# A decode kernel: query projection written to (head, batch) rows and spread by 4 products in place of 128, and a bias product from two bf16 parts

## Chip, cores, metric

One core of one Trainium2 chip. The metric is the device time of one execution in microseconds (us); lower is better. "Span" is the time from the first to the last instruction in a profile; it is some 1.5 us shorter than the device time.

## The reference, cut to what matters

```python
B, Sq, D = 4, 1, 640;  H, Sk, Dh = 32, 4096, 128;  F = 1728      # all bf16
q      = (layernorm(x) @ wq)  -> (B, H, 1, Dh)
scores = q . k_cache * Dh**-0.5                                   # k_cache, v_cache: (4, 32, 4096, 128)
o      = softmax(scores) . v_cache
h      = x + o.reshape(B, 1, H*Dh) @ wo
hid    = layernorm(h) @ w1 + b1
out    = h + mish(hid) @ w2
```

k_cache and v_cache are 134 MB each. With the weights, 283.35 MB have to be read once, and each byte is used for very little arithmetic.

## The kernel before

The caches are cut into 16 tiles of K and 16 of V (4 groups of 8 heads times 4 batches; 8.39 MB each, 128 partitions of 64 KB). They pass through three slots, A, B and C, in SBUF. Every large load is issued on one queue, by SyncE, as soon as its slot is free (x, b1 and one small piece of the weights are loaded through ScalarE's queue):

```python
def first_loads():
    load(sp, slot["C"][:, 0 : DC * H * Dh], ... A_wq ..., "wq", "WQ")    # 5.24 MB, in the slot of the first V
    ...
    k_load(0)                       # slot A
    k_load(1)                       # slot B

def sync_prog():
    for hg in range(NHG):
        ...
        sp.need(("PV", i - 1) if hg else ("qb", NHG - 1))    # the first V overwrites wq: wait for the projection
        v_load(i)
        sp.need(("F", i, NS - 1))   # fold of K tile i done: slot A is free
        k_load(i + 2)
        ...
```

VectorE multiplies a K tile by `q_bc` (q, repeated for all rows of its head), PE adds up over the head dimension (the "fold", with `ident` as weights), VectorE and ScalarE finish the scores, PE multiplies with V (`pv`).

The head of the program, which the change touches. wq is projected to `q_all`, rows (head group, batch), 1024 columns (8 heads by 128). Then, for each head group, batch and head, a product with a 0/1 matrix `sel` writes one head's q to the 16 rows that hold that head's keys:

```python
for h in range(2):
    for c in range(DC):
        for hg in range(NHG):
            o = hg * QN + h * 512
            mm(red[hg*QD : (hg+1)*QD, h, :], lnT[:, c, :], wq[:, c, o : o + 512], c == 0, c == DC - 1, ...)   # 40 products
pe.need(("qa", 0), ("qa", 1))            # two copies red -> q_all on ScalarE
for hg in range(NHG):
    for b in range(N):
        for g in range(G):               # 4 x 4 x 8 = 128 products
            mm(red[:, (2+hg) % 4, b*Dh : (b+1)*Dh], sel[r, b, SE - PG*g : SE - PG*g + P],
               q_all[r, g*Dh : (g+1)*Dh], g == 0, g == G - 1, ...)
# ScalarE: four copies red -> q_bc
```

The tail of the program, which the change touches as well. The bias b1 times the standard deviation is added to the first feed-forward product by one f32 product with an f32 identity, between the first and the second of three groups of w1 products:

```python
pe.need("cen")                           # centred h, bf16
for c0, c1 in zip(W1S, W1S[1:]):         # W1S = (0, 2, 4, 5)
    if c1 == DC - 1:
        pe.need("b1s")
        mm(red[:, 2, 0 : FC*N], ident_f[:, :], b1s[...], False, False)      # f32, 56 columns
    pe.need(("w1", c0))
    for j in ...: for c in range(c0, c1): mm(h1_ps[...], w1 piece, cen[:, c, :], ...)   # 28, 28 and 14 products
```

The softmax here doesn't subtract the row's maximum and nothing guards it: scores larger than these inputs give would overflow.

Of the kernel before, what the change touches and what calls it, by code (L numbers as in the profile page):

```python
# [7 lines left out]
FP32 = mybir.dt.float32  # L8
BF16 = mybir.dt.bfloat16
ACT = mybir.ActivationFunctionType  # L10
ALU = mybir.AluOpType
# [67 lines left out]
def kernel(  # L79
# [15 lines left out]
    N, _, D = A_x.shape  # L95
    _, H, Sk, Dh = A_k_cache.shape
    F = B_w1.shape[1]
    P = 128
    DC = D // P
    G = 8  # L100
    PG = P // G
    R = Sk // PG
    NS = 4
# [9 lines left out]
    CG = 4  # L113
# [59 lines left out]
    wq = slot["C"][:, 0 : DC * H * Dh].rearrange("p (c n) -> p c n", c=DC)  # L173
    x_bf = sb("x_bf", (N, D), BF16, setup, topC)
    ln1 = sb("ln1", (N, D), BF16, setup, topC)
    lnT = sb("lnT", (P, DC, QD), BF16, setup, topC)
    xT = sb("xT", (P, DC, N), BF16, setup, topC)
    q_all = sb("q_all", (P, QN), BF16, setup, topC)
    SE = P - PG
    sel_f = sb("sel_f", (P, N), FP32, setup, topC)  # L180
    sel = sb("sel", (P, N, SE + P), BF16, setup, topC)
    stats = sb("stats", (N, 2, nc.vector.BN_STATS_DIM), FP32, setup, topC)
    mv = sb("mv", (N, nc.vector.BN_AGGR_DIM), FP32, setup, topC)
    std = sb("std", (N, 1), FP32, setup, topC)
# [5 lines left out]
    tail = [sA + FM * D * 2]  # L190
    topA = sA + SLOT * 2
    ones_d = sb("ones_d", (P, P), FP32, tail, topA)
    ident_f = sb("ident_f", (P, P), FP32, tail, topA)
    zeros = sb("zeros", (P, OC), BF16, tail, topA)
    st = sb("st", (P, 2, DC, N), FP32, tail, topA)
    mu = sb("mu", (P, 2, N), FP32, tail, topA)
# [3 lines left out]
    std2 = sb("std2", (P, N), FP32, tail, topA)  # L200
    rstd = sb("rstd", (P, N), FP32, tail, topA)
    b1s = sb("b1s", (P, FC, N), FP32, tail, topA)
    h_hi = sb("h_hi", (P, DC, N), BF16, tail, topA)
    h_lo = sb("h_lo", (P, DC, N), BF16, tail, topA)
    act = sb("act", (P, FC, N), BF16, tail, topA)
# [90 lines left out]
    def sync_prog():  # L296
        for hg in range(NHG):
            i = hg * N
            if hg:
                sp.need(("PV", i - 2))  # L300
                k_load(i)
                sp.need(("F", i - 1, NS - 1))
                k_load(i + 1)
            sp.need(("PV", i - 1) if hg else ("qb", NHG - 1))
            v_load(i)
            sp.need(("F", i, NS - 1))
            k_load(i + 2)
            sp.need(("PV", i))
            v_load(i + 1)
            sp.need(("F", i + 1, NS - 1))  # L310
            k_load(i + 3)
            sp.need(("F", i + 2, NS - 1))
            v_load(i + 2)
            sp.need(("PV", i + 1))
            v_load(i + 3)
        sp.need(("F", NT - 1, NS - 1))
        for n, (q, j0, j1) in enumerate(WOS):
            load(
                sp, wo_sb[:, q, j0:j1, :],
                A_wo[q * QN : (q + 1) * QN, :].rearrange("(p j) n -> p j n", j=G)[:, j0:j1, :],  # L320
                ("wo", q, j0), f"W{n}",
            )
        w1_v = B_w1.rearrange("(p c) n -> p c n", c=DC)
        for k, (c0, c1) in enumerate(zip(W1S, W1S[1:])):
            load(sp, w1_sb[:, c0:c1, :], w1_v[:, c0:c1, :], ("w1", c0), f"W{len(WOS) + k}")
        sp.need(("PV", NT - 2))
        w2_v = B_w2[0 : FM * P, :].rearrange("(p j) n -> p j n", j=FM)
        for k, (j0, j1) in enumerate(zip(W2S, W2S[1:])):
            load(sp, w2_sb[:, j0:j1, :], w2_v[:, j0:j1, :], ("w2", j0), f"W{len(WOS) + len(W1S) - 1 + k}")
        store(sp, 0)  # L330
        leave(sp, 0)

    def pool_prog():
        g = nc.gpsimd
        po.do(lambda: g.memset(ident[:, :], 0.0), "id0", "PO")
        po.need("id0")
        po.do(
            lambda: g.affine_select(
                out=ident[:, :], in_=ident[:, :], compare_op=ALU.not_equal, fill=1.0, base=0,
                pattern=[[-1, P]], channel_multiplier=1,  # L340
            ),
            "ident", "PO",
        )
        po.do(lambda: g.memset(b1T[:, :], 0.0), "b1z", "PO")
        po.do(lambda: g.memset(lnT[:, :, :], 0.0), "lnz", "PO")
        po.do(lambda: g.memset(sel[:, :, :], 0.0), "selz", "PO")
        po.do(lambda: g.memset(selo[:, :, :], 0.0), "seloz", "PO")
        po.do(lambda: g.memset(ones[:, :], 1.0), "ones", "PO")
        po.need(("PV", NT - 2))
        po.do(lambda: g.memset(ones_d[:, :], 1.0 / D), "ones_d", "PO")  # L350
        po.do(lambda: g.memset(zeros[:, :], 0.0), "zeros", "PO")
        po.do(lambda: g.tensor_copy(out=ident_f[:, :], in_=ident[:, :]), "ident_f", "PO")

    def act_prog():
        a = nc.scalar
# [7 lines left out]
            ),  # L363
            "std", "AC",
        )
        for h in range(2):
            ac.need(("q", h))
            ac.do(
                lambda: a.copy(out=q_all[:, h * 512 : (h + 1) * 512], in_=red[:, h, :]),
                ("qa", h), "ACP",  # L370
            )
        for hg in range(NHG):
            ac.need(("qb", hg))
            ac.do(
                lambda: a.copy(
                    out=q_bc[:, hg, :, :].rearrange("p b d -> p (b d)"), in_=red[:, (2 + hg) % 4, :]
                ),
                ("qc", hg), "AC",
            )

        ac.need("ident")
# [52 lines left out]
    def dve_prog():  # L434
# [5 lines left out]
        for k in range(2):  # L440
# [3 lines left out]
        dv.need("ident")  # L444
        dv.do(
            lambda: v.tensor_reduce(
                out=sel_f[:, :],
                in_=ident[:, :].rearrange("p (h m) -> p m h", h=CG)[:, 0:N, :],
                axis=AX.X, op=ALU.add,
            ),  # L450
            "sel_f", DV,
# [28 lines left out]
            ),  # L480
            "selo", DVP,
        )
        dv.need("delta_f", "selz")
        dv.do(lambda: v.tensor_copy(out=hmask[:, :], in_=hmask_f[:, :]), "hmask", DV)
        dv.do(lambda: v.tensor_copy(out=delta[:, :], in_=delta_f[:, :]), "delta", DVP)
        dv.do(
            lambda: v.tensor_copy(
                out=sel[:, :, SE : SE + PG],
                in_=sel_f[:, :].unsqueeze(2).to_broadcast([P, N, PG]),
            ),  # L490
            "sel", DVP,
        )
# [8 lines left out]
            "ln1", DVP,  # L501
        )
        dv.need("tpl", "lnz")
        dv.do(lambda: v.tensor_copy(out=lnT[:, :, 0:N], in_=tpl[:, :, :]), "lnT", DVP)
        dv.need("tpx")
        dv.do(lambda: v.tensor_copy(out=xT[:, :, :], in_=tpx[:, :, :]), "xT", DVP)
        dv.do(lambda: v.memset(rsm[:, :, :], 1.0), ("rsm", -1), DVP)
        dv.need(("qc", NHG - 1), "hmask")

        def mult(i, s):  # L510
            hg, b = divmod(i, N)
# [109 lines left out]
        for k in range(2):  # L621
# [34 lines left out]
                out=b1s[:, :, :], in0=b1T[:, :].unsqueeze(2).to_broadcast([P, FC, N]),  # L656
                in1=std2[:, :].unsqueeze(1).to_broadcast([P, FC, N]), op=ALU.mult,
            ),
            "b1s", DVP,
        )  # L660
        dv.do(lambda: v.reciprocal(out=rstd[:, :], in_=std2[:, :]), "rstd", DV)
        dv.need("h_hi")
        dv.do(
            lambda: v.tensor_tensor(
                out=h_lo[:, :, :], in0=st[:, 0, :, :], in1=h_hi[:, :, :], op=ALU.subtract
            ),
            "h_lo", DVP,
        )
        dv.need("h1_ps", "rstd")
        dv.do(  # L670
# [59 lines left out]
    def pe_setup():  # L730
        pe.need("ident", "x", "delta", "ones")
        for c in range(DC):
            mm(
                tpx[:, c, :], x_bf[:, :].rearrange("n (p c) -> n c p", c=DC)[:, c, :],
                ident[0:N, 0:N], True, True, "tpx" if c == DC - 1 else None,
            )
        pe.need("ln1")
        for c in range(DC):
            mm(
                tpl[:, c, :], ln1[:, :].rearrange("n (p c) -> n c p", c=DC)[:, c, :],  # L740
                ident[0:N, 0:N], True, True, "tpl" if c == DC - 1 else None,
            )
        pe.need("xT")
        mm(y_full[:, 0 : DC * N], ident[:, :], xT[:, :, :].rearrange("p c n -> p (c n)"), True, False)
        pe.need("lnT", "wq")
        for h in range(2):
            for c in range(DC):
                for hg in range(NHG):
                    o = hg * QN + h * 512
                    mm(  # L750
                        red[hg * QD : (hg + 1) * QD, h, :], lnT[:, c, :], wq[:, c, o : o + 512],
                        c == 0, c == DC - 1,
                        ("q", h) if c == DC - 1 and hg == NHG - 1 else None,
                    )
        pe.need(("qa", 0), ("qa", 1))
        for hg in range(NHG):
            for b in range(N):
                for g in range(G):
                    r = slice(hg * QD, (hg + 1) * QD)
                    done = b == N - 1 and g == G - 1  # L760
                    mm(
                        red[:, (2 + hg) % 4, b * Dh : (b + 1) * Dh],
                        sel[r, b, SE - PG * g : SE - PG * g + P],
                        q_all[r, g * Dh : (g + 1) * Dh],
                        g == 0, g == G - 1, ("qb", hg) if done else None,
                    )

    def fold(i, s):
        t = slot[KS[i % N]][:, :].rearrange("p (r d) -> p r d", d=Dh)
# [76 lines left out]
    def pe_tail():  # L846
# [14 lines left out]
        l_mm(hg)  # L861
        wo_mm(1)
        a_mm(hg)
        pe.need("ident_f", ("e", NT - 1, NS - 1))
        mm(red[:, 2, 0 : FC * N], ident[:, :], zeros[:, 0 : FC * N], True, False)
        mm(y2_ps, ident[:, :], zeros[:, 0:OC], True, False)
        wo_mm(2)
# [8 lines left out]
            )  # L876
        pe.need("cen")
        for c0, c1 in zip(W1S, W1S[1:]):
            if c1 == DC - 1:
                pe.need("b1s")  # L880
                mm(
                    red[:, 2, 0 : FC * N], ident_f[:, :], b1s[:, :, :].rearrange("p j n -> p (j n)"),
                    False, False,
                )
            pe.need(("w1", c0))
            for j in [FM] + list(range(FM)):
                for c in range(c0, c1):
# [6 lines left out]
                        h1_ps[0 : (P if j < FM else FT), j, :], w, cen[:, c, :], False, done,  # L894
                        "h1_ps" if done else None,
                    )
        pe.need("h_lo")
        for part in (h_hi, h_lo):
            for k in range(CG):
                for c in range(DC):  # L900
# [89 lines left out]
```

## Time and profile before

663.92 us (median of 3 runs, 663.88 to 663.99); span 662.2 us.

| | before |
|---|---|
| busy share of the span: PE, VectorE, ScalarE | 60%, 61%, 6% |
| DMA, 36 to 636 us | share 1.00, 433 GB/s |
| q_bc complete / first product with K0 starts | 35.3 / 36.84 us |
| last half of the last V lands / its products start | 635.9 / 636.02 us |
| last piece of w2 lands / last result computed | 658.4 / 660.3 us |

Lines of the page of the profile. The first is busy time per engine. The next two cut the span into 40 slices: the clock granted to PE in tenths, and the busy share of the 16 DMA engines in tenths. Then come groups of instructions: line, engine, operation, output and inputs, count, busy time and mean ns, and after the second bar the idle time before them with what ended it.

```profile
...
PE 399.4 (60%) x2747; PEld 83.3 (13%) x1787; DVE 406.8 (61%) x252; ACT 41.6 (6%) x158; POOL 2.6 (0%) x14
...
PEclk9998698869659796869668778977965879786855
DMA  9999999999999999999999999999999999999997
...
L515 DVE TENSOR_TENSOR slotA<-slotA,q_bc 128x8192 bf16<-128x8192 bf16 x32 | 140.6, 4415 | 108.1 <-DMA slotA<-in_A_k_cache_dram 108.1
...
L708 PE MATMUL red<-q_all,sel 32*128 32x128 bf16 x128 | 12.5, 307 | 0.8 <-PEq L49 0.8
```

(The first clock record in this trace is at 46.8 us; the 9s that open its PEclk line stand for no record.) No compute engine is busy much more than 60% of the time, while the DMA engines are in the top tenth in every slice but the last. VectorE's products with K idle 108 us for the K tiles of slot A alone, and the profile puts all of it down to their DMA. The stretch from 36 to 636 us alone (columns: busy time of PE, PE weight load, VectorE, ScalarE, GpSimd, granted clock, DMA share, GB/s):

```profile
...
36.00:636.00 600.00, 359.24 (x2184) 50.30 (x1225) 398.61 (x213) 32.08 (x144) 0.61 (x3) 0.80 1.00 433
```

The Trainium skill ("DMA: Bandwidth & Descriptors", Specifications) gives 435 GB/s as the ceiling of the fabric; 433 over 600 us is within 0.5% of it.

Now the two places of the change. In the timeline (start, duration, engine, operation), the last copy to q_bc:

```profile
...
34.71 0.59 ACT L375 CAST q_bc<-red 128x512 bf16<-128x512 f32 x1 [2.38 <-PE red L708]
```

VectorE's first two products with K0, and what ended the idle time before them:

```profile
...
36.84 8.76 DVE L515 TENSOR_TENSOR slotA<-slotA,q_bc 128x8192 bf16<-128x8192 bf16 x2 [28.68 <-DMA slotA<-in_A_k_cache_dram]
```

The issue of the load of the first V (slot C) and of the third K (slot A):

```profile
...
34.70 0.33 SPq L250 DMA_DIRECT2D slotC<-in_A_v_cache_dram  x1
64.68 0.33 SPq L250 DMA_DIRECT2D slotA<-in_A_k_cache_dram  x1
```

q_bc was there 1.5 us before VectorE started; what it waited for was K0. In the tail, around the bias product (group of 28, bias weight load and product in two passes, groups of 28 + 14, and the step that takes the result):

```profile
...
636.02 3.60 PE L708 MATMUL pv<-slotC,e 128*32 128x512 bf16 x32 [3.16 <-PEq L49]
...
650.60 1.92 PE L708 MATMUL red<-cen,slotB 128*64 128x4 bf16 x28
...
652.32 0.54 PEld L708 LDWEIGHTS red<-b1s,ident_f 128*128 128x128 f32 x2
652.38 0.66 PE L708 MATMUL red<-b1s,ident_f 128*128 128x56 f32 x2
...
652.97 2.98 PE L708 MATMUL red<-cen,slotB 128*64 128x4 bf16 x42
...
655.99 0.22 DVE L671 TENSOR_TENSOR h<-red,rstd 128x56 f32<-128x56 f32 x1 [4.29 <-PE red L708]
```

The chain that ended last (start, duration, what) holds in one piece the three groups and the bias:

```profile
...
635.98 0.04 issue
...
650.60 5.36 PE red L708 x72
```

Everything on that chain before 635.98 us is waiting for data; from there it is compute.

### The profile page before, as it was taken

How to read it: one execution, taken by the hardware profiler on the slowest of the kernel's cores; microseconds unless marked ns; L12 is line 12 of the kernel's file. 1: busy time of each engine (PE TensorE's matmuls, PEld its weight loads, DVE VectorE, ACT ScalarE, POOL GpSimd, SP SyncE). 2: the span in 40 equal slices, each digit the busy share in tenths (PEclk: the TensorE clock that was granted, in tenths of full speed). 3: DMA queues.
4: the chain of work that ended last, by engine and by line, in shares of the span. 5: the costliest groups of instructions: out<-in, count | busy, mean ns of one | idle time of the engine just before them, and what ended most of it. 6: DMA issues, size and time to landing. Idle time of an engine off the chain costs nothing. (4 is left out here: it accounts for less than half of the span.)

```text
span 662.2 us, 5205 instructions
## 1 busy us (share of the span) xinstructions
PE 399.4 (60%) x2747; PEld 83.3 (13%) x1787; DVE 406.8 (61%) x252; ACT 41.6 (6%) x158; POOL 2.6 (0%) x14
## 2 busy tenths in 40 slices
PE   0957666557317595838307485828534757675877
PEld 0710010101101010101100010100110001010147
DVE  1067889486048778677219688948306798858612
ACT  0110000000000000000000000000000000000011
POOL 1000000000000000000000000000000000000000
PEclk9998698869659796869668778977965879786855
DMA  9999999999999999999999999999999999999997
GB/s 385 437 443 413 420 444 433 444 435 436 421 432 439 428 443 435 439 420 435 439 428 435 443 439 420 435 439 424 439 439 443 420 435 435 428 439 439 412 419 289
DMA packets 6978, 283.50 MB, mean 428 GB/s; under 512 B 1012, under 2 KB 1208, under 8 KB 2232
## 3 DMA queue, kind: packets, MB, share of 16 engines
q1 hardware_dynamic: 6640, 283.27, 99.0%
q8 instruction: 7, 0.11, 0.1%
q10 hardware_dynamic: 328, 0.09, 0.1%
q14 instruction: 3, 0.02, 0.0%
HBM read 283.35 MB, written 0.01 MB: 428 GB/s over the span
## 5 line engine op out<-in xcount | busy, mean ns | idle before, releaser
L515 DVE TENSOR_TENSOR slotA<-slotA,q_bc 128x8192 bf16<-128x8192 bf16 x32 | 140.6, 4415 | 108.1 <-DMA slotA<-in_A_k_cache_dram 108.1
L515 DVE TENSOR_TENSOR slotB<-slotB,q_bc 128x8192 bf16<-128x8192 bf16 x32 | 140.7, 4417 | 17.0 <-DMA slotB<-in_A_k_cache_dram 17.0
L526 DVE TENSOR_REDUCE s_f<-red 128x64 f32<-128x1024 f32 x64 | 78.0, 1219 | 97.6 <-PE red L718 97.6
L718 PE MATMUL red<-slotA,ident 128*128 128x512 bf16 x480 | 135.9, 446 | 0.0
L718 PE MATMUL red<-slotB,ident 128*128 128x512 bf16 x480 | 127.9, 426 | 0.0
L708 PE MATMUL red<-slotA,ident 128*128 128x512 bf16 x32 | 14.3, 447 | 117.2 <-PEq L49 117.2
L708 PE MATMUL pv<-slotC,e 128*32 128x512 bf16 x768 | 53.1, 437 | 37.0 <-PEq L49 34.0
L708 PE MATMUL red<-slotB,ident 128*128 128x512 bf16 x32 | 14.1, 441 | 87.7 <-PEq L49 87.7
L394 ACT ACTIVATE ex<-s_f 128x64 bf16<-128x64 f32 x64 | 16.4, 256 | 503.2 <-DVE s_f L526 503.2
L540 DVE TENSOR_TENSOR e<-ex,hmask 128x512 bf16<-128x512 bf16 x64 | 39.8, 683 | 0.0
L708 PEld LDWEIGHTS pv<-slotC,e 128*32 128x32 bf16 x768 | 22.7, 108 | 94.1 <-issue 80.5
L708 PEld LDWEIGHTS red<-slotA,ident 128*128 128x128 bf16 x32 | 3.2, 99 | 184.7 <-issue 184.6
L708 PEld LDWEIGHTS red<-slotB,ident 128*128 128x128 bf16 x32 | 3.2, 99 | 171.9 <-issue 171.9
L708 PEld LDWEIGHTS o_ps<-pv_sb,selo 128*32 128x32 f32 x136 | 13.9, 113 | 65.0 <-issue 64.8
L708 PE MATMUL o_ps<-pv_sb,selo 128*32 128x128 f32 x136 | 18.9, 284 | 0.0
L708 PE MATMUL pv<-slotA,e 128*32 128x512 bf16 x256 | 14.6, 380 | 0.3 <-PEq L49 0.3
L404 ACT COPY pv_sb<-pv 128x512 f32<-128x512 f32 x16 | 9.4, 586 | 68.4 <-PE pv L708 68.4
L708 PE MATMUL red<-q_all,sel 32*128 32x128 bf16 x128 | 12.5, 307 | 0.8 <-PEq L49 0.8
L708 PEld LDWEIGHTS red<-q_all,sel 32*128 32x128 bf16 x128 | 12.2, 142 | 1.7 <-issue 1.7
L394 ACT ACTIVATION_READ_ACCUMULATOR ex<-s_f 128x1 f32 x64 | 11.9, 186 | 0.0
L708 PEld LDWEIGHTS pv<-slotA,e 128*32 128x32 bf16 x256 | 6.7, 97 | 23.4 <-issue 17.5
L708 PE MATMUL red<-slotC,lnT 128*32 128x512 bf16 x40 | 4.5, 629 | 8.5 <-PEq L49 8.5
(96 smaller groups left out, 74.3 us busy)
## 6 DMA issues: line engine op xcount, KB each, us to landing
slotC<-in_A_v_cache_dram SPq DMA_DIRECT2D x2, 4096.0 KB, 39.1
slotC<-in_A_wq_dram SPq DMA_DIRECT2D x1, 5120.0 KB, 15.9
slotB<-in_A_wo_dram SPq DMA_DIRECT2D x3, 1280.0 KB, 15.7
slotB<-in_B_w_dram SPq DMA_DIRECT2D x2, 864.0 KB, 22.8
slotB<-in_A_wo_dram SPq DMA_DIRECT2D x1, 960.0 KB, 20.1
slotA<-in_B_w_dram SPq DMA_DIRECT2D x1, 960.0 KB, 25.1
slotA<-in_B_w_dram SPq DMA_DIRECT2D x1, 640.0 KB, 22.3
slotB<-in_B_w_dram SPq DMA_DIRECT2D x1, 432.0 KB, 24.2
```

The source lines that it names most:

```text
L394: lambda: a.activation(out=ex[:, sl], in_=s_f[:, sl], func=ACT.Exp, scale=SCALE, accum_out=rs[:, b, s : s + 1],),
L404: lambda: a.copy(out=pv_sb[:, :, :].rearrange("p r d -> p (r d)"), in_=pv[:, :]),
L515: lambda: v.tensor_tensor(out=t, in0=t, in1=q_bc[:, hg, b, :].unsqueeze(1).to_broadcast([P, RS, Dh]), op=ALU.mult,),
L526: lambda: v.tensor_reduce(out=s_f[:, s * RS : (s + 1) * RS], in_=red[:, k : k + 2, :].rearrange("p k (r c) -> p (k r) c", c=CW), axis=AX.X ...
L540: lambda: v.tensor_tensor(out=e[:, sl, :], in0=ex[:, sl].unsqueeze(2).to_broadcast([P, RS, G]), in1=hmask[:, :].unsqueeze(1).to_broadcast( ...
L708: lambda: nc.tensor.matmul(out_, lhsT=lhsT, rhs=rhs, start=start, stop=stop, skip_group_check=skip),
L718: return t.add_instruction(mybir.InstMatmult(name=nc.get_next_instruction_name(), engine=mybir.EngineType.PE, ins=[t.lower_ap(rhs), t.lowe ...
```

## The change

Its intent: get q_bc ready sooner, with far fewer instructions, and replace an f32 product on PE's path in the tail by two cheap bf16 ones. lnT is kept with zeros on both sides, so that a shifted view of it writes the 4 batches of head g to the rows (g, b) of a quarter of PSUM. After 40 products of the old size, `q_all` holds rows (quarter, head within its group, batch) and 512 columns (4 head groups by 128). One 128 by 128 product per batch then spreads all heads and all head groups at once. The bias is split as b1s = b1_hi + b1_lo, two bf16 numbers that together carry about 16 bits of it, and moves behind the second group of w1. The diff, cut:

```diff
-    lnT = sb("lnT", (P, DC, QD), BF16, setup, topC)
+    lnT = sb("lnT", (P, DC, 2 * QD - N), BF16, setup, topC)
...
-            sp.need(("PV", i - 1) if hg else ("qb", NHG - 1))
+            sp.need(("PV", i - 1) if hg else ("qb", N - 1))
...
-        for h in range(2):
+        GK = G // CG
+        for r in range(GK):
             for c in range(DC):
-                for hg in range(NHG):
-                    o = hg * QN + h * 512
+                for k in range(CG):
+                    g = k * GK + r
                     mm(
-                        red[hg * QD : (hg + 1) * QD, h, :], lnT[:, c, :], wq[:, c, o : o + 512],
+                        red[k * QD : (k + 1) * QD, 0, :], lnT[:, c, QD - N * (g + 1) : 2 * QD - N * (g + 1)],
+                        wq[:, c, :].rearrange("p (h g d) -> p g h d", g=G, d=Dh)[:, g, :, :],
...
-        for hg in range(NHG):
-            for b in range(N):
-                for g in range(G):
...
+        for b in range(N):
+            mm(
+                red[:, (1 + b) % 4, :], sel[:, b * G : (b + 1) * G, :].rearrange("p g q -> p (g q)"),
+                q_all[:, :], True, True, ("qb", b),
+            )
...
+        dv.do(lambda: v.tensor_copy(out=b1_hi[:, :, :], in_=b1s[:, :, :]), "b1_hi", DV)
...
+                out=b1_lo[:, :, :], in0=b1s[:, :, :], in1=b1_hi[:, :, :], op=ALU.subtract
...
-            if c1 == DC - 1:
-                pe.need("b1s")
-                mm(
-                    red[:, 2, 0 : FC * N], ident_f[:, :], b1s[:, :, :].rearrange("p j n -> p (j n)"),
-                    False, False,
-                )
+            if c1 == DC:
+                pe.need("b1_lo")
+                for part in (b1_hi, b1_lo):
+                    mm(
+                        red[:, 2, 0 : FC * N], ident[:, :], part[:, :, :].rearrange("p j n -> p (j n)"),
+                        False, False,
+                    )
```

Left out: one copy to q_all less on ScalarE, the wider `sel` on VectorE, a memset and a cast less on GpSimd.

More of the change, by code (lines that the diff above doesn't have):

```diff
@@ L175 @@
     ln1 = sb("ln1", (N, D), BF16, setup, topC)
-    lnT = sb("lnT", (P, DC, QD), BF16, setup, topC)
+    lnT = sb("lnT", (P, DC, 2 * QD - N), BF16, setup, topC)
     xT = sb("xT", (P, DC, N), BF16, setup, topC)
-    q_all = sb("q_all", (P, QN), BF16, setup, topC)
-    SE = P - PG
-    sel_f = sb("sel_f", (P, N), FP32, setup, topC)
-    sel = sb("sel", (P, N, SE + P), BF16, setup, topC)
+    q_all = sb("q_all", (P, NHG * Dh), BF16, setup, topC)
+    sel_f = sb("sel_f", (P, N, G), FP32, setup, topC)
+    sel = sb("sel", (P, BG, PG), BF16, setup, topC)
     stats = sb("stats", (N, 2, nc.vector.BN_STATS_DIM), FP32, setup, topC)
@@ L192 @@
     ones_d = sb("ones_d", (P, P), FP32, tail, topA)
-    ident_f = sb("ident_f", (P, P), FP32, tail, topA)
     zeros = sb("zeros", (P, OC), BF16, tail, topA)
@@ L202 @@
     b1s = sb("b1s", (P, FC, N), FP32, tail, topA)
+    b1_hi = sb("b1_hi", (P, FC, N), BF16, tail, topA)
+    b1_lo = sb("b1_lo", (P, FC, N), BF16, tail, topA)
     h_hi = sb("h_hi", (P, DC, N), BF16, tail, topA)
@@ L345, in pool_prog @@
         po.do(lambda: g.memset(lnT[:, :, :], 0.0), "lnz", "PO")
-        po.do(lambda: g.memset(sel[:, :, :], 0.0), "selz", "PO")
         po.do(lambda: g.memset(selo[:, :, :], 0.0), "seloz", "PO")
@@ L351, in pool_prog @@
         po.do(lambda: g.memset(zeros[:, :], 0.0), "zeros", "PO")
-        po.do(lambda: g.tensor_copy(out=ident_f[:, :], in_=ident[:, :]), "ident_f", "PO")
     def act_prog():
@@ L365, in act_prog @@
         )
-        for h in range(2):
-            ac.need(("q", h))
-            ac.do(
-                lambda: a.copy(out=q_all[:, h * 512 : (h + 1) * 512], in_=red[:, h, :]),
-                ("qa", h), "ACP",
-            )
-        for hg in range(NHG):
-            ac.need(("qb", hg))
+        ac.need("q")
+        ac.do(lambda: a.copy(out=q_all[:, :], in_=red[:, 0, :]), "qa", "ACP")
+        for b in range(N):
+            ac.need(("qb", b))
             ac.do(
                 lambda: a.copy(
-                    out=q_bc[:, hg, :, :].rearrange("p b d -> p (b d)"), in_=red[:, (2 + hg) % 4, :]
+                    out=q_bc[:, :, b, :],
+                    in_=red[:, (1 + b) % 4, :].rearrange("p (h d) -> p h d", d=Dh),
                 ),
-                ("qc", hg), "AC",
+                ("qc", b), "AC",
             )
@@ L446, in dve_prog @@
             lambda: v.tensor_reduce(
-                out=sel_f[:, :],
-                in_=ident[:, :].rearrange("p (h m) -> p m h", h=CG)[:, 0:N, :],
+                out=sel_f[:, :, :],
+                in_=ident[:, :].rearrange("p (k g b) -> p b g k", k=CG, b=N),
                 axis=AX.X, op=ALU.add,
@@ L482, in dve_prog @@
         )
-        dv.need("delta_f", "selz")
+        dv.need("delta_f")
         dv.do(lambda: v.tensor_copy(out=hmask[:, :], in_=hmask_f[:, :]), "hmask", DV)
@@ L487, in dve_prog @@
             lambda: v.tensor_copy(
-                out=sel[:, :, SE : SE + PG],
-                in_=sel_f[:, :].unsqueeze(2).to_broadcast([P, N, PG]),
+                out=sel[:, :, :], in_=sel_f[:, :, :].rearrange("p b g -> p (b g)").unsqueeze(2).to_broadcast([P, BG, PG]),
             ),
@@ L503, in dve_prog @@
         dv.need("tpl", "lnz")
-        dv.do(lambda: v.tensor_copy(out=lnT[:, :, 0:N], in_=tpl[:, :, :]), "lnT", DVP)
+        dv.do(lambda: v.tensor_copy(out=lnT[:, :, QD - N : QD], in_=tpl[:, :, :]), "lnT", DVP)
         dv.need("tpx")
@@ L507, in dve_prog @@
         dv.do(lambda: v.memset(rsm[:, :, :], 1.0), ("rsm", -1), DVP)
-        dv.need(("qc", NHG - 1), "hmask")
+        dv.need(("qc", N - 1), "hmask")
         def mult(i, s):
@@ L658, in dve_prog @@
             ),
-            "b1s", DVP,
+            "b1s", DV,
         )
+        dv.need("b1s")
+        dv.do(lambda: v.tensor_copy(out=b1_hi[:, :, :], in_=b1s[:, :, :]), "b1_hi", DV)
         dv.do(lambda: v.reciprocal(out=rstd[:, :], in_=std2[:, :]), "rstd", DV)
@@ L666, in dve_prog @@
             ),
-            "h_lo", DVP,
+            "h_lo", DV,
+        )
+        dv.need("b1_hi")
+        dv.do(
+            lambda: v.tensor_tensor(
+                out=b1_lo[:, :, :], in0=b1s[:, :, :], in1=b1_hi[:, :, :], op=ALU.subtract
+            ),
+            "b1_lo", DVP,
         )
@@ L745, in pe_setup @@
         pe.need("lnT", "wq")
-        for h in range(2):
+        GK = G // CG
+        for r in range(GK):
             for c in range(DC):
-                for hg in range(NHG):
-                    o = hg * QN + h * 512
-                    mm(
-                        red[hg * QD : (hg + 1) * QD, h, :], lnT[:, c, :], wq[:, c, o : o + 512],
-                        c == 0, c == DC - 1,
-                        ("q", h) if c == DC - 1 and hg == NHG - 1 else None,
-                    )
-        pe.need(("qa", 0), ("qa", 1))
-        for hg in range(NHG):
-            for b in range(N):
-                for g in range(G):
-                    r = slice(hg * QD, (hg + 1) * QD)
-                    done = b == N - 1 and g == G - 1
-                    mm(
-                        red[:, (2 + hg) % 4, b * Dh : (b + 1) * Dh],
-                        sel[r, b, SE - PG * g : SE - PG * g + P],
-                        q_all[r, g * Dh : (g + 1) * Dh],
-                        g == 0, g == G - 1, ("qb", hg) if done else None,
-                    )
+                for k in range(CG):
+                    g = k * GK + r
+                    mm(
+                        red[k * QD : (k + 1) * QD, 0, :], lnT[:, c, QD - N * (g + 1) : 2 * QD - N * (g + 1)],
+                        wq[:, c, :].rearrange("p (h g d) -> p g h d", g=G, d=Dh)[:, g, :, :],
+                        r == 0 and c == 0, r == GK - 1 and c == DC - 1,
+                        "q" if r == GK - 1 and c == DC - 1 and k == CG - 1 else None,
+                    )
+        pe.need("qa", "sel")
+        for b in range(N):
+            mm(
+                red[:, (1 + b) % 4, :], sel[:, b * G : (b + 1) * G, :].rearrange("p g q -> p (g q)"),
+                q_all[:, :], True, True, ("qb", b),
+            )
     def fold(i, s):
@@ L863, in pe_tail @@
         a_mm(hg)
-        pe.need("ident_f", ("e", NT - 1, NS - 1))
+        pe.need("zeros", ("e", NT - 1, NS - 1))
         mm(red[:, 2, 0 : FC * N], ident[:, :], zeros[:, 0 : FC * N], True, False)
@@ L878, in pe_tail @@
         for c0, c1 in zip(W1S, W1S[1:]):
-            if c1 == DC - 1:
-                pe.need("b1s")
-                mm(
-                    red[:, 2, 0 : FC * N], ident_f[:, :], b1s[:, :, :].rearrange("p j n -> p (j n)"),
-                    False, False,
-                )
+            if c1 == DC:
[4 more added lines that the diff above has]
+                        False, False,
+                    )
             pe.need(("w1", c0))
@@ L896, in pe_tail @@
                     )
-        pe.need("h_lo")
+        pe.need("h_lo", "h_hi")
         for part in (h_hi, h_lo):
```

## The prediction

> **What bounds the kernel now.** The DMA stream. In the page's 40 slices the DMA engines are in the top tenth in all but the last; the stretch view gives a DMA share of 1.00 and 433 GB/s from 36 to 636 us. The Trainium skill ("DMA: Bandwidth & Descriptors", Specifications) gives 435 GB/s as fabric ceiling; the slices, 413 to 444, agree. PE and DVE are busy 60% and 61%; DVE's products with q_bc idle 125 us waiting for K from HBM (page, costliest groups).
> The chain that ended last starts only at 636.0, when the last half of V has landed, and is compute from there to 662.2. The last part of w2 lands at 658.4, so the tail can gain at most about 1.5 us before it meets the DMA again.
>
> **Head.** Now wq lands at 16.8 us; 40 projection products (4.5 us busy) end at 21.4; two ACT copies (0.59 each); 128 spreading products, 12.5 us busy, end at 34.7; the last q_bc copy ends at 35.3. The first product with K0 starts at 36.84, after waiting for K0's DMA, not for q_bc. Changed: the same 40 products, one copy, 4 full products (estimate 0.25 to 0.45 us each, from this trace's 512-column products at 0.22 to 0.44), 4 copies. q_bc is ready near 25 us, 10 us earlier; K0 still lands at 36.5, so DVE idles as before. V0's load over wq is issued near 23.5 instead of 34.70, behind K0 and K1 (K1 lands near 56). The skill (same page, "Queues, rings and completion order") says that each DMA engine consumes descriptors in ring order; here loads on this queue land in order of issue. No engine gets work it would have lacked. Gain on the critical path: 0. Larger casts on DVE and a larger memset on POOL (tenths of a us) lie 8 us ahead of wq's landing.
>
> **Middle.** No code changes. Clock windows may shift, but releases have several us of queued load behind them (shortest landing 25.2 us after issue, against 19.4 for 8.39 MB at 433 GB/s). 0.
>
> **Tail.** The f32 bias product (0.66 us busy in two passes, some 0.5 between its neighbours, 652.5 to 653.0) becomes two bf16 ones. Two like them (the zero products) take 0.29 on the chain; estimate 0.2. The bias moves behind the second w1 group, to about 654.4; b1_lo is ready by 652.2 (b1s at 651.5, then four small DVE operations of 0.15 to 0.2 us): no wait. w1's last part has landed at 653.4. Gain 0.3 us; what follows is unchanged, and the last w2 part (658.4) is used near 659.
>
> **Prediction: 663.6 us, 662.6 to 664.4 (8 in 10); faster by over 2%: 1%; within 2%: 98%; slower: 1%.**
>
> **Right if** the 128 products fall to 4 with under 2 us busy; q_bc's last copy ends at 24 to 26 us; the first K product still starts at 36.5 to 37.2, its idle time put down to K0's DMA; V0 is issued near 23.5 but lands as before; K2's issue stays near 64.7; V's last half lands at 635.9 ± 0.7; the chain from cen to h is 0.2 to 0.4 us shorter.
>
> **Wrong if** K0's landing moves (something in the head held it, not the stream); if the earlier V0 load competes with K0 and K1 instead of queueing, delaying the first product; if the tail's granted clock (0.50) changes, worth up to 1.5 us until the DMA binds; if the bias products wait for b1_lo; or if the stream's rate moves by 0.1%, worth 0.65 us.

## The result, and the profile after

663.26 us (median of 4 runs, 663.09 to 663.35) against 663.90 us (4 runs, 663.63 to 663.99) before. The ratio is 0.9991 with a 95% interval of 0.9973 to 1.0008: the same. The output is correct.

| | before | after |
|---|---|---|
| q_bc complete | 35.3 us | 24.8 us |
| load of the first V issued | 34.70 us | 23.38 us |
| first product with K0 starts | 36.84 us | 36.50 us |
| DMA, 36 to 636 us | 433 GB/s | 433 GB/s |
| products with the last half of V start | 636.02 us | 636.06 us |
| from the first w1 product to the step `h` | 5.39 us | 4.93 us |
| span | 662.15 us | 661.73 us |

The same lines of the page after. The 128 spreading products are gone from the costliest groups, PE is 13 us less busy, and the DMA line is the same:

```profile
...
PE 386.2 (58%) x2622; PEld 70.3 (11%) x1663; DVE 407.5 (62%) x254; ACT 40.7 (6%) x157; POOL 1.7 (0%) x12
...
PEclk9768697979759697958767888787875879797965
DMA  9999999999999999999999999999999999999997
...
L509 DVE TENSOR_TENSOR slotA<-slotA,q_bc 128x8192 bf16<-128x8192 bf16 x32 | 140.6, 4416 | 106.4 <-DMA slotA<-in_A_k_cache_dram 106.4
```

```profile
...
36.00:636.00 600.00, 358.87 (x2184) 50.14 (x1224) 398.68 (x213) 30.95 (x143) 0.38 (x2) 0.79 1.00 433
```

The head in the timeline: all four copies to q_bc, the issue of V0's load, and VectorE's first product with K0. It still waits for K0, 28.35 us instead of 28.68:

```profile
...
22.73 2.05 ACT L369 CAST q_bc<-red 128x512 bf16<-128x512 f32 x4 [0.56 <-PE red L711]
...
23.38 0.33 SPq L250 DMA_DIRECT2D slotC<-in_A_v_cache_dram  x1
...
36.50 4.42 DVE L509 TENSOR_TENSOR slotA<-slotA,q_bc 128x8192 bf16<-128x8192 bf16 x1 [28.35 <-DMA slotA<-in_A_k_cache_dram]
```

The tail: the products with V's last half, the last 40 products with wo, two groups of 28, the two bias weight loads and products, the last 14, and `h`:

```profile
...
636.06 3.56 PE L711 MATMUL pv<-slotC,e 128*32 128x512 bf16 x32 [5.78 <-PEq L49]
...
647.52 1.73 PE L711 MATMUL y_ps<-a_t,slotB 128*128 128x4 bf16 x40 [0.53 <-DMA slotB<-in_A_wo_dram]
...
650.63 3.77 PE L711 MATMUL red<-cen,slotB 128*64 128x4 bf16 x56
...
654.21 0.13 PEld L711 LDWEIGHTS red<-b_hi,ident 128*128 128x128 bf16 x1
654.25 0.21 PE L711 MATMUL red<-b_hi,ident 128*128 128x56 bf16 x1
654.26 0.10 PEld L711 LDWEIGHTS red<-b_lo,ident 128*128 128x128 bf16 x1
654.28 0.23 PE L711 MATMUL red<-b_lo,ident 128*128 128x56 bf16 x1
...
654.44 1.08 PE L711 MATMUL red<-cen,slotB 128*64 128x4 bf16 x14
...
655.56 0.22 DVE L674 TENSOR_TENSOR h<-red,rstd 128x56 f32<-128x56 f32 x1 [3.50 <-PE red L711]
```

And two pieces of the chain. The first is new and is taken up below (the chain now runs over a piece of wo); the second is the stretch of w1, 4.91 us instead of 5.36:

```profile
...
625.30 22.09 DMA slotB<-in_A_wo_dram
...
650.63 4.91 PE red L711 x72
```

So the head won 10.5 us for q_bc, none of which appears in the span, and the tail won 0.45 us, which does (0.42 us in this pair of profiles). Part of the 10.5 us is chance: in four other profiles with the old head (bias_only, f32_late, hilo_early and quarters_old_head, below) q_bc was complete at 33.0 to 33.2 us, and with the new head at 23.5 to 25.1, so the change itself is worth some 8 to 10 us. Two things had to be tested. First: is it really the stream that swallows the head's gain, or only that K0 happens to land late? Second: is 0.45 us in the tail the whole effect, or does the head add to it (the medians differ by 0.64)?

### The profile page after: what moved, and what is told of

Same layout as the page of the kernel before. It is cut to its first block, busy times and chain, and to the rows that moved or that the text cites. A ratio compares the mean times of both kernels' runs of the same rounds, so it can differ in the third digit from the quotient of the medians.

```text
span 661.7 us, 4955 instructions
## 1 busy us (share of the span) xinstructions
PE 386.2 (58%) x2622; PEld 70.3 (11%) x1663; DVE 407.5 (62%) x254; ACT 40.7 (6%) x157; POOL 1.7 (0%) x12
## 5 line engine op out<-in xcount | busy, mean ns | idle before, releaser
L721 PE MATMUL red<-slotA,ident 128*128 128x512 bf16 x480 | 137.9, 452 | 0.0
L721 PE MATMUL red<-slotB,ident 128*128 128x512 bf16 x480 | 126.3, 423 | 0.0
L711 PE MATMUL red<-slotA,ident 128*128 128x512 bf16 x32 | 14.4, 452 | 128.7 <-PEq L49 128.7
L711 PE MATMUL red<-slotB,ident 128*128 128x512 bf16 x32 | 14.2, 443 | 86.4 <-PEq L49 86.4
L711 PE MATMUL y_ps<-a_t,slotB 128*128 128x4 bf16 x160 | 7.0, 180 | 0.7 <-DMA slotB<-in_A_wo_dram 0.7
```

Source lines behind the costliest of these rows:

```text
L711: lambda: nc.tensor.matmul(out_, lhsT=lhsT, rhs=rhs, start=start, stop=stop, skip_group_check=skip),
L721: return t.add_instruction(mybir.InstMatmult(name=nc.get_next_instruction_name(), engine=mybir.EngineType.PE, ins=[t.lower_ap(rhs), t.lowe ...
```

## The experiments

Ten experiments followed, nine new kernels and the changed one again; all gave correct results. Two attempts to shorten the chain behind `h` (a power and a division on VectorE in place of the reciprocal) did not compile and were dropped.

### 1. The two halves of the change alone

`head_only`: the new query projection with the old bias. `bias_only`: the old projection with the new bias.

```diff
 # head_only, against the kernel after
-            if c1 == DC:
-                pe.need("b1_lo")
-                for part in (b1_hi, b1_lo): ...
+            if c1 == DC - 1:
+                pe.need("b1s")
+                mm(red[:, 2, 0 : FC * N], ident_f[:, :], b1s[...], False, False)
 # bias_only: the reverse edit, against the kernel before
```

> The new query projection with the old f32 bias product. My theory: the head is hidden behind K0's landing (36.7 us before, 36.4 after) and behind the stream, so the time stays that of before, 663.8 to 663.95 in the median, although q_bc is ready some 10 us earlier and V0 is issued near 23.4 instead of 34.7. The rival, that part of the measured 0.6 us comes from the head (earlier V0 load, fewer instructions to fetch), expects 663.2 to 663.6.

> The old query projection with the new bias products. My theory: the whole gain of the change, 663.2 to 663.5, and the stretch from cen to h at 4.9 to 5.0 us on the chain instead of 5.4. The rival (head) expects 663.5 to 663.9.

Measured, 5 rounds, 9 runs of before on the same chip with a median of 663.96 us: head_only 663.79 (663.57 to 663.84), ratio 0.9995 (0.9982 to 1.0009); bias_only 663.42 (663.24 to 663.84), ratio 0.9991 (0.9978 to 1.0005). Both medians fall where the theory put them (head_only 0.01 us below its window), but the intervals overlap: by time alone this is not decided. The profiles decide it. From the first w1 product to `h`, head_only takes 5.38 us:

```profile
...
650.54 1.92 PE L702 MATMUL red<-cen,slotB 128*64 128x4 bf16 x28
...
655.92 0.22 DVE L665 TENSOR_TENSOR h<-red,rstd 128x56 f32<-128x56 f32 x1 [4.29 <-PE red L702]
```

and bias_only 4.94 us:

```profile
...
650.81 3.77 PE L717 MATMUL red<-cen,slotB 128*64 128x4 bf16 x56
...
655.75 0.22 DVE L680 TENSOR_TENSOR h<-red,rstd 128x56 f32<-128x56 f32 x1 [3.50 <-PE red L717]
```

Then everything from the start of V's last half to the end of the span, which is the tail without the stream ahead of it, in all twelve profiles:

| kernel | bias | head | last pv half starts | span | difference |
|---|---|---|---|---|---|
| before | f32 | old | 636.02 | 662.15 | 26.13 |
| head_only | f32 | new | 635.96 | 662.09 | 26.12 |
| f32_late (below) | f32, moved | old | 636.00 | 662.07 | 26.07 |
| quarters_old_head (below) | f32 | old | 636.04 | 662.13 | 26.09 |
| quarters_new_head (below) | f32 | new | 636.26 | 662.36 | 26.10 |
| spread_half_more (below) | f32 | old, slower | 635.98 | 662.31 | 26.33 |
| spread_twice (below) | f32 | old, slower | 641.82 | 668.07 | 26.25 |
| after | bf16 | new | 636.06 | 661.73 | 25.67 |
| after_again | bf16 | new | 636.46 | 662.14 | 25.67 |
| bias_only | bf16 | old | 636.25 | 661.91 | 25.67 |
| hilo_early (below) | bf16, old place | old | 636.18 | 661.87 | 25.69 |
| after_wo_split (below) | bf16 | new | 636.22 | 661.86 | 25.65 |

The tail takes 26.07 to 26.33 us with the f32 product and 25.65 to 25.69 with the two bf16 ones, whichever head is in front of it. (The two longest f32 tails, of the runs with more spreading products, were held up by pieces of wo or w1 that landed later.) The column with the start, where the stream lets the tail begin, varies by 0.5 us without spread_twice, with no order by head or bias: the same program, the changed kernel, started its tail at 636.06 in one profile and at 636.46 in the other. That scatter is as large as the effect, and it is what the times mix in.

### 2. The changed kernel once more

> The changed kernel once more, with five rounds on one chip. Theory (only the bias product counts): 0.4 to 0.5 us under the kernel before, 663.2 to 663.6, as bias_only; the stretch from cen to h at 4.9 us again. If the head adds something, the distance to before is larger than bias_only's.

Measured: 663.49 us (663.30 to 663.78) against 663.85 (9 runs), ratio 0.9992 (0.9979 to 1.0006); from w1 to `h` 4.93 us. The distance of the medians is 0.36 us here, 0.54 for bias_only and 0.64 in the first result. Nothing is left over that would have to come from the head; the smaller distance of the same kernel here says that part of the 0.64 was scatter.

### 3. The data type or the place

```diff
 # f32_late, against before: only the place
-            if c1 == DC - 1:
+            if c1 == DC:
 # hilo_early, against bias_only: only the place, back again
-            if c1 == DC:
+            if c1 == DC - 1:
```

> Before, with the single f32 bias product only moved from behind the first to behind the second group of w1 products. If the data type is what gains (my theory), the time stays 663.8 to 664.0, since PE waits for b1s in neither place. If the place is what gains (in the old place the f32 weight load waits for b1s, or delays the group behind it), it is 663.4 or less.

> The old query projection, two bf16 bias products in the old place, behind the first group. b1_lo was ready at 652.1 in the profile after, the first group ends at 652.5, so my theory expects no wait and the same gain as bias_only: 663.2 to 663.5. If the move was needed to hide the longer chain to b1_lo, it shows a wait of PE for b1_lo and 0.1 to 0.4 us less gain.

Measured: f32_late 663.69 us, ratio 1.0000 (0.9987 to 1.0014), from w1 to `h` 5.34 us; hilo_early 663.55 us, ratio 0.9995 (0.9981 to 1.0009), 4.95 us. So the type is worth 0.44 us in the old place (5.39 against 4.95) and 0.41 in the new one (5.34 against 4.93); the place is worth 0.05 us with f32 and 0.02 with bf16. PE waited for b1_lo in neither place. The medians lie 0.11 and 0.05 us outside the windows I had stated; with intervals of 0.9 us to either side they could not have told such amounts apart. The profiles do. First the two lines of f32_late (the first w1 products, then `h`), then those of hilo_early:

```profile
...
650.57 3.77 PE L708 MATMUL red<-cen,slotB 128*64 128x4 bf16 x56
...
655.90 0.22 DVE L671 TENSOR_TENSOR h<-red,rstd 128x56 f32<-128x56 f32 x1 [4.25 <-PE red L708]
```

```profile
...
650.75 1.93 PE L717 MATMUL red<-cen,slotB 128*64 128x4 bf16 x28
...
655.71 0.22 DVE L680 TENSOR_TENSOR h<-red,rstd 128x56 f32<-128x56 f32 x1 [3.51 <-PE red L717]
```

Where f32 spends it is visible in the lines of before and after: the f32 bias is recorded as two weight loads (0.54 us together) and two products, the two bf16 loads took 0.13 and 0.10 us. The Trainium skill ("TensorE: Matmul & The Clock Gate", Weight-path perf modes) states that the fast weight load is on for 128 weights of a type that isn't FP32; 0.27 us for each f32 load against 0.10 to 0.13 is in keeping with that, but no run separates a slower load from the second load and product. From the start of the bias product to the start of the next group it was 0.59 us (652.38 to 652.97) and is now 0.19 (654.25 to 654.44).

### 4. How much slack the head has

If the stream alone counts, the head may also become slower without cost, up to the moment when the queue runs empty. Before, with some or all of the 128 spreading products done a second time:

```diff
         for hg in range(NHG):
-            for b in range(N):
-                for g in range(G):
-                    done = b == N - 1 and g == G - 1
+            for rep in range(2 if hg < 2 else 1):        # spread_half_more;  range(2): spread_twice
+              for b in range(N):
+                for g in range(G):
+                    done = last rep and b == N - 1 and g == G - 1
```

> Before, with half of the 128 spreading products done a second time (same result), so that q_bc is ready about 6.2 us later, near 41.5, and V0 is issued near 40.9. Theory 1 (only the DMA stream counts, and it has V0's and K1's bytes queued until about 73): DVE starts about 4.8 us later, yet K2's load is issued near 69, before the stream runs dry; time unchanged, 663.7 to 664.2. Theory 2 (DVE's first product is on the critical path, with 1.5 us of slack before K0): 668 to 669.

> Before, all 128 spreading products done twice: q_bc ready near 47.8. Theory 1: V0 is issued near 47, before K1 has landed (54 to 56); K2's load is issued near 75.7, 1 to 2 us after the first DMA engines ran out of V0: a small hole in the stream and 665 to 668. Theory 2: 674 to 675.

spread_half_more: 664.02 us (663.82 to 665.83) against 663.78, ratio 1.0012 (0.9995 to 1.0028). q_bc was complete at 39.2 us, not at 41.5, because of the clock: it was recorded as 1.00 from 21.4 to 24.8 us, and the first repeated group of products took 4.4 us, the second, at 0.50, 6.4. (My estimate came from before, where no spreading product took less than 0.26 us, against 0.21 here: that reads as the low clock from the start, although the page shows 9s. That is also the chance in the 10.5 us above.) And now VectorE waited for q_bc:

```profile
...
39.23 8.76 DVE L515 TENSOR_TENSOR slotA<-slotA,q_bc 128x8192 bf16<-128x8192 bf16 x2 [31.07 <-ACT q_bc L375]
```

That is 2.4 us later than before, less than the intended 4.8, and the time did not follow. K2's load was issued at 66.81 us instead of 64.68. A theory in which VectorE's start sets the time asks for 2.4 us more with this smaller dose, 666.2; the median is 664.02, and the interval allows 1.9 us more at most. One of the four runs took 665.83 us; it has no profile, so why is open.

spread_twice: 669.55 us (668.80 to 671.24), ratio 1.0091 (1.0072 to 1.0109); span 668.1. VectorE started at 47.23 us, 10.4 us late, and the time grew by 5.8. Neither number of mine holds: Theory 2 wanted 674 or more, Theory 1 665 to 668. The issues by SyncE of K2, of V1 and of V2 show why:

```profile
...
73.77 0.33 SPq L250 DMA_DIRECT2D slotA<-in_A_k_cache_dram  x1
94.32 0.33 SPq L250 DMA_DIRECT2D slotC<-in_A_v_cache_dram  x1
...
135.12 0.33 SPq L250 DMA_DIRECT2D slotA<-in_A_v_cache_dram  x1
```

K2's load was issued when the first DMA engines were just finishing the load before it (their first completion count came at 73.88 us; in before there were 9.0 us between the two, 64.68 and 73.67). The same happened twice more: V1 was issued 0.6 us before K2's first completion, V2 0.1 us after K3's. From the first completion counts of each load against those in before, the stream fell behind by 1.96 us at K2 (0.21 of it already at V0), by 3.42 at V1, by 5.48 at V2, and from there on it never lost more than another 0.7. I had expected one hole; there were three, because a late VectorE releases several slots late in turn before it catches up. The step of my estimate that failed is that it took the first hole to make up for the whole lateness. The first hole in the stretch from 72 to 78 us, in before

```profile
...
72.00:78.00 6.00, 5.20 (x14) 0.10 (x1) 4.99 (x2) 0.00 (x0) 0.00 (x0) 0.54 0.86 371
```

in spread_half_more

```profile
...
72.00:78.00 6.00, 3.07 (x8) 0.10 (x1) 6.00 (x2) 0.00 (x0) 0.00 (x0) 0.50 0.86 371
```

and in spread_twice

```profile
...
72.00:78.00 6.00, 1.74 (x9) 0.00 (x0) 4.22 (x6) 0.35 (x2) 0.00 (x0) 1.00 0.67 240
```

371, 371 and 240 GB/s: 131 GB/s less over 6 us is 0.79 MB, or 1.8 us of the stream at 433 GB/s. (Why even the intact stream shows 0.86 here was not looked into; the figures of short stretches scatter, from 20 to 36 us the view gives 456 GB/s in before.) So the time grew by what the stream lost (5.48 us and at most 0.7 more, against 5.8), and a late VectorE as such cost nothing. Note that the loss began before the margin was used up: issues 0.11 and 0.6 us ahead cost 1.75 and 1.47 us, one 0.12 us late cost 2.03. Margin and cost add up to 1.9 to 2.1 us each time, so an estimate from these three is that a load has to be issued about 2 us before the first completion of the one ahead; nothing between 0.6 and 3.7 us was measured.

### 5. K0 landing early

If it were only K0's late landing that hid the head, an earlier K0 would bring the head's gain to light. K0 in four parts, each with its own semaphore:

```diff
     def k_load(i):
+        if i == 0:
+            for s in range(NS):
+                q = slice(s * RS * Dh, (s + 1) * RS * Dh)
+                load(sp, slot["A"][:, q], tiles(A_k_cache, i)[:, q], ("K0", s), f"KQ{s}")
+            return
...
-            dv.need(("K", i))
+            dv.need(("K", i) if i else ("K0", s))
```

> Before, with K0 loaded in four parts of a quarter each, every product waiting for its own part. K0's first quarter lands near 22, so now q_bc (35.3) is what the first product waits for: DVE starts at 35.4. Time unchanged, 663.6 to 664.2, since the stream is the same.

> The same four parts of K0, with the new query projection and the old bias. Now the new head shows on DVE: it starts near 25, some 10 us before the kernel with the old head, paced by the quarters. If K0's landing alone hid the head, this is several us faster than with the old head. My theory: the stream still sets the time; within 0.3 us of the other, 663.6 to 664.2.

With the old head VectorE's first products now wait for q_bc, which was complete at 33.2 us and not at the 35.3 that I had taken from before (the clock again):

```profile
...
33.21 8.76 DVE L520 TENSOR_TENSOR slotA<-slotA,q_bc 128x8192 bf16<-128x8192 bf16 x2 [23.06 <-ACT q_bc L380]
```

and with the new head they start 8.6 us earlier:

```profile
...
24.64 8.76 DVE L514 TENSOR_TENSOR slotA<-slotA,q_bc 128x8192 bf16<-128x8192 bf16 x2 [14.29 <-ACT q_bc L374]
```

Times: 663.88 us (663.68 to 664.12) with the old head, 664.04 (663.79 to 664.31) with the new, ratios 1.0002 (0.9985 to 1.0018) and 1.0004 (0.9987 to 1.0021). VectorE starts 12 us before its start in the kernel before, and the span does not move: K0's landing was the first thing to hide the head, the stream is the second, and it suffices alone.

### 6. Trying to go further in the tail

The changed kernel's chain ran over a piece of wo, on its way to `st` (VectorE's copy of the finished sum x + o @ wo out of PSUM): PE waited 0.53 us for it and then had 40 products to do. In before, at half the clock from 630.5 us to the end, PE was late by itself and did not wait there; in the profile after the clock was full from 639.4 to 642.9, PE came 0.9 us earlier, and waited. st began at the same time in both (649.27 and 649.29). So I loaded this piece in smaller parts:

```diff
-WOS = [...] + [(NHG - 1, 0, G - 2), (NHG - 1, G - 2, G)]
+WOS = [...] + [(NHG - 1, 0, 3), (NHG - 1, 3, 6), (NHG - 1, 6, G)]
```

> The changed kernel with the last quarter of wo loaded in pieces of 3, 3 and 2 of its 8 parts in place of 6 and 2. In the profile after, PE waited 0.53 us for the piece of 6 (landed 647.39) and then had 40 products of 1.75 us to do. If that landing is what the tail hangs on, PE starts them up to 0.7 us earlier and st comes 0.2 to 0.5 us earlier: 662.8 to 663.2. If the clock in this stretch is low, so that PE is late by itself as in the profile before, nothing changes: 663.2 to 663.5.

Measured: 663.47 us (663.26 to 663.60) against 663.49 for the changed kernel in the same rounds; ratio to before 0.9992 (0.9979 to 1.0006). That is above the 662.8 to 663.2 that I expected, although the clock was full again from 640.4 to 643.8 us. From the products with wo on:

```profile
...
645.39 3.63 PE L711 MATMUL y_ps<-a_t,slotB 128*128 128x4 bf16 x80
649.06 0.18 DVE L607 COPY st<-y_ps 128x20 f32<-128x20 f32 x1 [3.88 <-PE y_ps L711]
...
650.62 3.90 PE L711 MATMUL red<-cen,slotB 128*64 128x4 bf16 x56 [0.29 <-DMA slotB<-in_B_w_dram]
...
655.69 0.22 DVE L674 TENSOR_TENSOR h<-red,rstd 128x56 f32<-128x56 f32 x1 [3.87 <-PE red L711]
```

The 80 products now run through. st comes 12.84 us after the start of V's last half, 0.39 us earlier than after's 13.23, as expected. But the w1 products then wait 0.29 us for the first part of w1, and the chain runs over the second part, which landed at 652.54. The difference to the end of the span is 25.65 us against 25.67. The gain was given back to the next landing. No version that beats the changed kernel came out of this.

## Why the prediction was right

The measured 663.26 us (and 663.49 in the repetition) lies in the range of 662.6 to 664.4, and the mechanism was the predicted one. The time alone proves little: the kernel before, at 663.90, lies in that range too. Point by point:

- *The DMA stream bounds the kernel.* Shown (a clause of the prediction is cut: it put the slices at 413 to 444 GB/s and called that agreement with the ceiling, but three lie lower, at 385, 412 and 289, and some lie above 435; what agrees is 433 over 600 us): 433 GB/s before and after, no gain from a head made faster (head_only) nor from VectorE starting 12 us earlier (quarters_new_head), no loss resolved from one made slightly slower, and a loss equal to the holes once the queue ran dry (spread_twice).
- *Head: 0.* Shown. q_bc at 24.8 us (predicted 24 to 26), V0 issued at 23.38 (23.5), first product with K0 at 36.50 (36.5 to 37.2), K2 issued at 63.88 (64.7), V's last half in use at 636.06. The statement that loads on this queue land in order held in all twelve profiles. The Trainium skill ("DMA: Bandwidth & Descriptors", Queues, rings and completion order) promises less: descriptors are consumed in ring order on each DMA engine, but a later one may finish its write before an earlier one. V0, issued 11.3 us earlier, landed within 0.4 us of its old time (74.95 and 75.33).
- *Tail: 0.3 us.* Right in kind, too small: 0.45 us, outside the stated 0.2 to 0.4. The mis-sized term is the old f32 product, put down as "some 0.5 between its neighbours"; from its start to the start of the next group it was 0.59. The new pair was predicted at 0.2 and took 0.19. The remaining 0.05 or so is the place (experiment 3).
- *The tail can gain at most about 1.5 us before it meets the DMA again.* Too generous. That bound looked only at the last piece of w2. The pieces of wo and w1 land just as close to their use: with full clock in 639.4 to 642.9 us PE came up against wo, and with wo in smaller parts against w1. For steps ahead of st, the room found was nothing. The clause that a change of the tail's clock would be worth up to 1.5 us fell with it as far as it was tried: ahead of st the clock did change, and gained nothing (25.67 us for the tail of after and after_again, with a full stretch, and 25.67 and 25.69 for bias_only and hilo_early, without). Behind st it was 0.50 in all twelve profiles, so what a full clock would do there stays open.
- *Middle: several us of queued load.* Right, and now with a number from the other side: in before, 9.0, 7.2 and 8.0 us lie between the issues of K2, V1 and V2 and the first completion of the load ahead of them; the smallest such distance among all K and V tiles is 3.8 us.

What stays open: whether the two kernels' times differ by 0.45 us. The profiles say so for the tail; the intervals of the times, about 0.17% to either side, do not resolve it. And why the stream reaches V's last half at moments up to 0.5 us apart in runs of one program was not looked into.

## What to carry to other kernels

Before making a stage faster, ask what its result is needed for and whether that has arrived: here the 10 us or so won in the head were hidden by K0's landing, and behind that by a stream that never ran empty. On a stream-bound kernel the lever is not when an engine starts but whether a load is always queued; count the us between issuing a load and the end of the one before it, since a slow stage cost nothing here while 3.7 us or more were left; at 0.6 us it already cost 1.5, and then it costs at several releases in turn. And where runs scatter by as much as the effect, measure a stretch of the profile that starts behind the scatter: the tail, taken from its own start, separated 26.07 to 26.33 from 25.65 to 25.69 us without one overlap.

## What the Trainium skill lacked or had wrong

- "TensorE: Matmul & The Clock Gate", What's actually happening, says that about 3.4 us of sustained activity bring PE to its full clock. In the tail they did not: in the kernel before, PE was busy 6.94 of the 7.00 us from 640 to 647, long enough to hold a whole such window wherever it starts, at a granted clock of 0.50, and the clock stayed at 0.50 to the end. The durations agree with the record: the eight products for `o_ps` took 1.91 us there and 1.06 at the full clock in after. Most of the products in this stretch have 4 columns. In after, products of 512 columns had filled 636.06 to 639.44 us just before the clock rose at 639.44. The section does not say which kind of activity counts.

```profile
...
640.00:643.00 3.00, 3.00 (x42) 2.67 (x41) 0.00 (x0) 1.54 (x2) 0.00 (x0) 0.50 1.02 432
643.00:647.00 4.00, 3.94 (x86) 3.83 (x85) 1.78 (x4) 0.00 (x0) 0.00 (x0) 0.50 1.00 419
```

- "DMA: Bandwidth & Descriptors" lacks how far ahead a load must be queued to keep the stream whole. Here issues 3.8 us and more ahead of the previous load's first completion (all K and V tiles of before) left the stream at 433 GB/s, and three issues between 0.6 us ahead and 0.1 us behind cost 1.5 to 2.0 us each (about 2 us ahead would do by the estimate in experiment 4).
- The same page, Specifications, lists about 358 GB/s as the limit from HBM for one core, without a condition in the table; 433 GB/s were read over 600 us here, with one core at work (further down the page names the other core's traffic as the condition).
